# Cross-attention with a snake MLP on one core: batch 4's load, pack and transpose moved forward in a hand-written order, and one square moved to VectorE

## The chip, the cores and the metric

The kernel runs on one core of a Trainium2 chip. The metric is the device time of one execution in microseconds (us), lower being better. The core has five engines that work side by side, each through its own instructions in order: PE (TensorE, matmuls), ACT (ScalarE), DVE (VectorE), POOL (GpSimd) and SP (SyncE, which here only issues DMA transfers). Sixteen DMA engines move the data. An instruction that needs another engine's result waits for it on a semaphore.

## What is computed

Cut to what matters, for B = 8 batches, H = 8 heads, S = 512 tokens, Ns = 32 state rows, D = 64:

```python
scores = scale * np.matmul(x, state.transpose(0, 1, 3, 2))
a = softmax(scores);   xread = np.matmul(a, state)
scores2 = scale * np.matmul(state, x.transpose(0, 1, 3, 2))
a2 = softmax(scores2); sread = np.matmul(a2, x)
attn = np.concatenate([xread, sread], axis=2)      # heads side by side: 4352 rows of 512
h = attn @ w_in                                     # 512 x 2048
s = np.sin(alpha * h)
out = (h + s * s / (alpha + 1e-09)) @ w_out         # 2048 x 512
```

The kernel works in bf16 with float32 accumulation. For `xread` it folds the state into `w_in` (a matrix M for each batch), so that the attention weights, transposed, are multiplied by M directly.

## The kernel before

The whole kernel is a class of small steps and one long string, `ORDER`, that lists them by hand. A step such as `sq.1.13.G` calls the method `sq` with the arguments 1, 13 and "G". The order of the string is the order of the instructions on every engine: each engine takes its own steps from it, and waits where a step needs something that isn't there. Nothing else sets an order. The framework adds the semaphores.

The steps, with t or b for the batch (t = 8 stands for the state rows of all batches), f for one of 16 blocks of 128 columns of the hidden layer:

- `lx.b.0.1`: POOL issues the DMA that loads x of batch b, 512 KB after its cast to bf16, into a tile `xnat` (pool `xpool`, 3 slots, used from batch 1 on).
- `pk.b.0.V`, `pk.b.1.V`: VectorE copies one half of `xnat` into `xp` (5 slots) in another layout. `td.b`: SP issues the DMA transpose of `xp` into `xT` (2 slots). Batch 1 is transposed on PE instead (`xt`, `xc`).
- `sc.b.g`: PE multiplies `xT` with the state into scores; `ex` takes their exponent on ACT; `rs`, `rr` sum and invert on VectorE; `nm` multiplies on POOL, giving the weights A; `ad.b`: SP issues the DMA transpose of A into AT.
- `w`, `cs`, `rc`, `xs`: the second attention (PE, then VectorE). `m` and `me`: M on PE, and its copies to SBUF.
- `h.t.f.bank`: PE multiplies M and AT into one PSUM bank (2 matmuls). `si`: sine on ACT. `sq.t.f.E`: the square on engine E, V for VectorE, A for ACT, G for POOL. `gt`: VectorE multiplies it with 1/alpha and adds h, and so frees the bank of h.
- `o.t.st.f0.f1`: PE multiplies blocks f0 to f1 of gT with w_out for a quarter st of the rows, accumulating in a bank. `oc.t.st.E`: the copy out of that bank. `os.t.st`: SP issues the store.

There are eight PSUM banks, and each `h`, `o`, `sc`, `w` and `m` names the bank it takes; PE has to wait until the bank's last reader is done. A block is the stretch in which a batch's 16 `h` and their squares run. The DMA transposes and the stores share SP's instruction stream, in the order of the string; the loads of x share POOL's with the squares and `nm`.

The change touches lines 52, 62, 64, 69 and 70 of the string. Four places of it, as they were:

```
si.1.13 h.1.15.2 sq.1.3.G gt.1.6 os.0.1 o.0.2.15.16 oc.0.0.A h.1.5.4 sq.1.13.G oc.0.2.V si.1.15
me.2.0.0.V sc.3.1.2 me.2.0.1.A o.1.1.12.13 o.1.3.9.10 xs.0.0 o.1.3.10.11 ex.3.0 o.1.1.13.16 ex.3.1
rr.3.1 h.2.1.3 oc.1.3.V nm.3.1.0.4.G h.2.2.4 h.2.8.1 os.1.3 h.2.3.7 lx.4.0.1 ad.3 si.2.2 o.1.0.0.3.2
sq.2.7.G gt.2.5 o.2.3.1.2 os.1.0 o.2.3.2.3 si.2.6 h.2.10.5 pk.4.1.V pk.4.0.V o.2.3.3.4 sq.2.6.A
o.2.3.4.5 gt.2.7 h.2.11.6 td.4 si.2.10 h.2.12.2 gt.2.6 si.2.11 o.2.0.2.3 sq.2.10.G o.2.0.3.4
```

The multiplication helper `mul` is line 201, so squares on VectorE and POOL, and `nm`, show under L201 in the profile; the copies show under the line of their step. L587 is `o`, L537 `h` (L552 in batch 0, L543 for the state rows), L399 `sc`, L560 `si`, L569 a square on ACT, L576 `gt`, L348 `pk`, L275 the load `lx`, L389 `td`, L440 `ad`, L602 the store.

Of the kernel before, what the change touches and what calls it, by code (L numbers as in the profile page):

```python
# [71 lines left out]
o.2.3.6.7 si.2.13 o.2.0.5.6 sq.2.15.G gt.2.12 o.2.0.6.8 si.2.14 o.2.3.7.9 sq.2.13.A o.2.3.9.10
gt.2.15 sq.2.14.G o.2.0.8.11 gt.2.13 o.2.0.11.12 sc.4.0.5 sc.4.1.6 gt.2.14 o.2.3.10.12 ex.4.0
o.2.3.12.13 w.1.2 cs.1 o.2.0.12.13 rc.1 o.2.3.13.15 ex.4.1 o.2.3.15.16 m.3.0.4.1.3.5 rs.4.0 oc.2.3.A
o.2.0.13.14 me.3.1.0.A o.2.0.14.15 os.2.3 me.3.0.0.V o.2.1.0.1.6 me.3.0.1.A o.2.1.1.2 o.2.0.15.16
rr.4.0 rs.4.1 o.2.1.2.3 me.3.1.1.A nm.4.0.0.4.G h.3.1.0 oc.2.0.A o.2.1.3.4 rr.4.1 xs.1.0
m.3.2.3.4.1.5 si.3.1 nm.4.1.0.4.G os.2.0 xs.1.1 h.3.0.7 me.3.2.0.V h.3.2.2 ad.4 me.3.3.0.V o.2.1.4.6
lx.5.0.1 o.2.2.0.1.3 me.3.3.1.V si.3.2 o.2.2.1.3 si.3.0 h.3.6.1 sq.3.1.V sq.3.2.G me.3.2.1.V
h.3.14.5 si.3.6 o.2.2.3.4 gt.3.1 o.2.2.4.5 sq.3.0.G si.3.14 o.2.2.5.7 gt.3.2 o.2.2.7.8 sq.3.6.A
o.2.2.8.9 h.3.8.4 sq.3.14.G gt.3.0 h.3.5.0 si.3.8 gt.3.6 h.3.15.2 si.3.5 o.2.2.9.10 sq.3.8.G gt.3.14  # L80
o.2.2.10.11 h.3.9.7 si.3.15 h.3.7.1 si.3.9 sq.3.5.G gt.3.8 o.2.2.11.13 si.3.7 h.3.10.5 sq.3.9.G
o.2.2.13.14 sq.3.15.A gt.3.5 o.2.2.14.15 h.3.4.4 si.3.10 gt.3.15 o.2.1.6.7 sq.3.7.G o.2.1.7.8 si.3.4
o.2.2.15.16 o.2.1.8.10 sq.3.10.A gt.3.9 o.2.1.10.11 sq.3.4.G gt.3.7 o.2.1.11.13 oc.2.2.A o.2.1.13.14
gt.3.10 o.2.1.14.16 os.2.2 h.3.3.0 gt.3.4 oc.2.1.A h.3.12.2 si.3.3 pk.5.1.V o.3.2.0.1.7 os.2.1
m.4.2.1.3.5.6 pk.5.0.V si.3.12 sq.3.3.V td.5 o.3.3.0.1.4 me.4.2.1.V me.4.2.0.A o.3.2.1.2 sq.3.12.G
o.3.3.1.2 me.4.3.0.A o.3.2.2.3 gt.3.3 o.3.3.2.3 h.3.11.1 me.4.3.1.A gt.3.12 h.4.10.3 si.3.11 h.4.9.5
si.4.10 h.4.12.0 sq.3.11.V h.4.11.6 si.4.9 gt.3.11 sq.4.10.G o.3.2.3.5 si.4.12 o.3.2.5.7 sq.4.9.A
o.3.2.7.8 gt.4.10 sq.4.12.G o.3.2.8.10 si.4.11 o.3.2.10.11 gt.4.9 o.3.3.3.5 sq.4.11.A o.3.3.5.6
gt.4.12 o.3.3.6.8 m.4.0.2.1.3.5 gt.4.11 o.3.3.8.9 me.4.1.1.V me.4.0.1.A h.3.13.0 me.4.0.0.A h.4.8.6
me.4.1.0.V h.4.15.1 si.3.13 h.4.2.5 si.4.8 sq.3.13.V h.4.1.2 lx.6.0.1 si.4.2 gt.3.13 o.3.2.11.12  # L90
o.3.1.0.2.3 si.4.15 o.3.1.2.3 sq.4.8.V o.3.1.3.4 sq.4.2.G si.4.1 gt.4.8 o.3.3.9.12 sq.4.15.A h.4.3.0
sq.4.1.G gt.4.2 o.3.3.12.13 h.4.13.6 si.4.3 gt.4.15 o.3.3.13.15 si.4.13 sq.4.3.G o.3.3.15.16 gt.4.1
h.4.6.5 oc.3.3.A o.3.2.12.13 h.4.5.1 sq.4.13.G si.4.6 gt.4.3 os.3.3 h.4.14.2 si.4.5 o.3.0.0.1.4
sq.4.6.G o.3.2.13.14 gt.4.13 si.4.14 o.3.0.1.4 sq.4.5.A h.4.4.0 sq.4.14.G gt.4.6 o.3.0.4.5 h.4.0.6
si.4.4 gt.4.5 o.3.1.4.6 si.4.0 sq.4.4.G gt.4.14 o.3.2.14.16 w.2.5 sq.4.0.A pk.6.1.V o.3.1.6.7
oc.3.2.A h.4.7.1 pk.6.0.V gt.4.4 sc.5.0.2 td.6 si.4.7 o.3.1.7.8 sc.5.1.7 gt.4.0 o.3.1.8.9 o.3.0.5.6
ex.5.0 sq.4.7.G o.3.0.6.8 o.3.1.9.11 os.3.2 o.3.0.8.9 gt.4.7 o.3.0.9.12 cs.2 ex.5.1 rs.5.0
m.5.0.0.6.1.2 o.3.0.12.13 rr.5.0 me.5.0.0.A rs.5.1 o.4.3.0.1.7 nm.5.0.0.4.G o.3.0.13.14 me.5.0.1.A
o.3.0.14.15 rr.5.1 o.3.1.11.12 me.5.1.1.V o.3.1.12.13 me.5.1.0.A nm.5.1.0.4.G o.4.3.1.3 rc.2
o.3.0.15.16 o.4.3.3.4 o.3.1.13.14 oc.3.0.A ad.5 o.3.1.14.15 xs.2.0 m.6.0.0.6.2.1 xs.2.1 o.4.3.4.5  # L100
me.6.1.1.V me.6.1.0.A sc.6.1.4 os.3.0 sc.6.0.5 me.6.0.1.A o.4.3.5.6 me.6.0.0.V o.4.3.6.7 ex.6.0
o.4.3.7.8 o.4.0.0.1.2 o.3.1.15.16 ex.6.1 rs.6.0 w.3.1 oc.3.1.A cs.3 rr.6.0 m.5.2.6.0.5.4 rs.6.1
nm.6.0.0.4.G os.3.1 o.4.3.8.9 me.5.2.0.A me.5.2.1.V o.4.0.1.2 o.4.3.9.10 me.5.3.0.A o.4.3.10.11
rr.6.1 o.4.2.0.1.3 rc.3 nm.6.1.0.4.G o.4.2.1.2 me.5.3.1.A h.5.8.6 o.4.3.11.12 xs.3.1 h.5.9.0 si.5.8
ad.6 xs.3.0 o.4.0.2.3 o.4.3.12.14 o.4.2.2.4 h.5.4.5 si.5.9 o.4.3.14.15 sq.5.8.V h.5.3.4 si.5.4
gt.5.8 o.4.2.4.5 sq.5.9.G h.5.0.1 si.5.3 o.4.3.15.16 o.4.0.3.4 si.5.0 sq.5.4.G o.4.2.5.6 oc.4.3.V
o.4.2.6.8 sq.5.3.A gt.5.9 h.5.1.6 os.4.3 sq.5.0.G h.5.5.7 gt.5.4 si.5.1 o.4.2.8.10 si.5.5 gt.5.3
h.5.2.0 sq.5.1.G o.4.2.10.11 gt.5.0 o.4.2.11.12 si.5.2 h.5.14.5 lx.7.0.1 sq.5.5.A gt.5.1 h.6.3.4
o.4.2.12.13 si.5.14 gt.5.5 o.4.2.13.14 sq.5.2.G o.4.0.4.5 o.5.0.0.1.1 si.6.3 o.4.2.14.15 h.6.6.6
sq.5.14.A sq.6.3.G gt.5.2 o.4.0.5.6 h.5.13.7 si.6.6 gt.5.14 o.4.0.6.8 si.5.13 sq.6.6.G o.4.0.8.9  # L110
gt.6.3 o.4.0.9.11 sq.5.13.A o.4.0.11.12 h.6.2.0 gt.6.6 h.5.12.5 si.6.2 gt.5.13 o.4.2.15.16 h.6.4.4
si.5.12 sq.6.2.G o.4.0.12.13 oc.4.2.V o.4.0.13.14 si.6.4 o.4.0.14.15 o.4.1.0.1.6 os.4.2 o.4.1.1.2
sq.5.12.A gt.6.2 sq.6.4.G o.5.0.1.3 o.4.0.15.16 gt.5.12 h.5.10.7 oc.4.0.A o.4.1.2.3 gt.6.4 o.4.1.3.4
si.5.10 o.4.1.4.5 os.4.0 o.4.1.5.6 pk.7.1.V o.4.1.6.7 sq.5.10.A o.4.1.7.8 pk.7.0.V o.4.1.8.10 td.7
gt.5.10 m.6.2.3.0.5.2 o.4.1.10.11 me.6.3.0.V me.6.3.1.A o.4.1.11.12 h.5.7.4 me.6.2.1.A me.6.2.0.V
h.5.11.7 si.5.7 h.5.15.2 si.5.11 h.5.6.5 sq.5.7.V h.6.15.0 si.5.15 gt.5.7 sq.5.11.G o.4.1.12.13
o.5.2.0.1.3 si.5.6 o.5.2.1.3 si.6.15 sq.5.15.G o.4.1.13.14 gt.5.11 o.4.1.14.16 sq.5.6.A h.6.11.4
sq.6.15.G oc.4.1.V h.6.1.7 si.6.11 gt.5.15 o.5.2.3.4 os.4.1 h.6.0.6 si.6.1 sq.6.11.G gt.5.6
o.5.0.3.5 si.6.0 o.5.0.5.6 w.4.2 sq.6.1.A gt.6.15 sq.6.0.G o.5.0.6.7 gt.6.11 o.5.0.7.8 o.5.2.4.5
sc.7.1.5 gt.6.1 sc.7.0.0 o.5.2.5.7 ex.7.0 gt.6.0 o.5.0.8.10 o.5.2.7.8 o.5.1.0.2.4 o.5.0.10.11  # L120
h.6.14.7 ex.7.1 h.6.13.6 rs.7.0 cs.4 si.6.14 rs.7.1 o.5.1.2.4 o.5.0.11.12 rr.7.1 o.5.0.12.13 rc.4
o.5.2.8.9 nm.7.1.0.4.G h.6.10.0 o.5.0.13.14 si.6.13 xs.4.1 o.5.2.9.10 sq.6.14.G o.5.2.10.11 xs.4.0
si.6.10 o.5.2.11.13 h.6.7.5 sq.6.13.A rr.7.0 nm.7.0.0.4.G o.5.2.13.15 si.6.7 h.6.12.2 sq.6.10.A
gt.6.14 gt.6.13 o.5.1.4.5 ad.7 sq.6.7.G o.5.1.5.7 si.6.12 gt.6.10 o.5.1.7.10 sq.6.12.A gt.6.7
o.5.1.10.11 o.5.0.14.15 o.5.1.11.12 gt.6.12 o.5.0.15.16 h.6.5.7 oc.5.0.A o.6.2.0.1.6 h.6.9.0 si.6.5
# [538 lines left out]
```

The softmax here doesn't subtract the row's maximum and nothing guards it: scores larger than these inputs give would overflow.

## Time and profile before

| | |
|---|---|
| time, median of 3 runs | 220.75 us (220.71 to 222.56) |
| span of the profiled execution | 221.2 us |
| busy: PE, ACT, DVE, POOL | 97%, 78%, 73%, 48% |
| lx.4 issued on POOL, for how long | at 63.71 us, 0.94 us |
| pk.4.1 and pk.4.0 on DVE | at 71.73 us, two copies in 0.76 us |
| td.4 issued on SP | at 72.55 us, 1.71 us |
| first scores of batch 4 on PE | at 76.97 us |
| sq.1.13 on POOL | ends at 46.40 us |
| loads of x, from issue to landing | 5.9 least, 7.7 median, 19.6 most |
| transposes into xT, the same | 4.2, 4.3, 5.5 |
| transposes into AT, the same | 3.0, 3.1, 6.8 |

The profile records one execution. Its page gives each engine's busy time, a picture of 40 slices, the chain of waits (followed back from the last instruction to what released each step), and groups of instructions with their mean duration. Other views list who waited for whom, the instructions in order of time (start, duration, engine, line, operation, how many), and the busy time of each engine in chosen stretches. PE's ends are modelled, and weight loads (PEld) overlap with matmuls. Where like instructions follow each other directly, the timeline merges them into one row with a count. A few matmul records are missing.

### The profile page before, as it was taken

The page shows a single profiled execution, that of the slowest core. Times are in us where ns is not written, and L with a number is a line of the kernel's source. Part 1 is how long each engine was busy: PE and PEld are TensorE (multiplying, and loading weights), DVE is VectorE, ACT ScalarE, POOL GpSimd, SP SyncE. Part 2 cuts the span into 40 slices and gives each one's busy share as a digit, 9 for nine tenths or more (in the row PEclk, how much of TensorE's full clock was granted, in tenths as well). Part 3 has the DMA queues.
Part 4 walks back from the last instruction along what each step waited for, and adds up shares of the span by engine and source line. Part 5 has one row for each costly group of instructions (what it writes and reads, how often), then busy time and mean ns, then how long its engine had stood idle before and what let it go on. Part 6 is the DMA issues. An engine that isn't in the chain of part 4 may idle for free.

```text
span 221.2 us, 4330 instructions
## 1 busy us (share of the span) xinstructions
PE 215.7 (97%) x1619; PEld 106.0 (48%) x1619; DVE 162.4 (73%) x286; ACT 173.5 (78%) x297; POOL 107.1 (48%) x115
## 2 busy tenths in 40 slices
...
GB/s 172 198 206 204 205 203 87 174 199 73 119 127 158 96 50 150 44 190 61 81 41 125 126 95 94 108 117 17 47 99 0 98 47 47 0 50 95 1 142 96
DMA packets 38052, 23.48 MB, mean 106 GB/s; under 512 B 20992, under 2 KB 33680, under 8 KB 38032
## 3 DMA queue, kind: packets, MB, share of 16 engines
...
q8 instruction: 12, 0.20, 0.4%
...
## 4 chain that ended last, share of the span: by engine, by line
PE 93%; ACT 3%; DMA 2%; SPq 0%; issue 0%
PE o_ps L587 54%; PE h_ps L537 22%; PE m_ps L488 4%; PE h_ps L543 3%; PE h_ps L552 3%; DMA x<-in_x_dram 2%; PE s_ps L399 2%; PE warm_ps L303 2%; PE w_ps L450 2%; PE w_ps L461 1%; PE x_ps L361 1%; ACT L226 1%; ACT s L560 1%; ACT M L496 1%; PE x_ps L376 0%; PE st_ps L333 0%
## 5 line engine op out<-in xcount | busy, mean ns | idle before, releaser
L587 PE MATMUL o_ps<-w_out_sb,gT 128*128 128x512 bf16 (+2 forms) x560 | 137.7, 373 | 0.0
L576 DVE SCALAR_TENSOR_TENSOR gT<-s,inva_sb,h_ps 128x512 bf16<-128x512 bf16 (+1 forms) x144 | 96.6, 714 | 18.8 <-POOL s L201 9.6
L201 POOL TENSOR_TENSOR s<-s 128x512 bf16<-128x512 bf16 (+1 forms) x76 | 76.7, 1021 | 65.9 <-ACT s L560 62.4
L560 ACT ACTIVATE s<-h_ps,alpha_sb 128x512 bf16<-128x512 f32 (+1 forms) x144 | 88.8, 671 | 10.5 <-PE h_ps L543 4.3
L587 PEld LDWEIGHTS <-gT 128*128 128x128 bf16 x560 | 52.3, 98 | 60.3 <-issue 5.0
L537 PE MATMUL h_ps<-AT,M 128*128 128x512 bf16 x224 | 60.8, 379 | 0.0
L537 PEld LDWEIGHTS <-M 128*128 128x128 bf16 x224 | 21.7, 98 | 25.9 <-issue 0.4
L569 ACT ACTIVATE s<-s 128x512 bf16<-128x512 bf16 (+1 forms) x53 | 31.4, 595 | 0.8
L201 POOL TENSOR_TENSOR A<-E,rR 128x512 bf16<-128x512 bf16 x16 | 16.6, 1048 | 25.7 <-ACT o_sb L595 12.7
L595 ACT COPY o_sb<-o_ps 128x512 f32<-128x512 f32 (+2 forms) x24 | 13.7, 571 | 16.6 <-PE o_ps L587 16.5
L496 ACT CAST M<-m_ps 128x512 bf16<-128x512 f32 x35 | 18.6, 594 | 8.2 <-PE m_ps L488 8.1
L496 DVE CAST M<-m_ps 128x512 bf16<-128x512 f32 x29 | 18.9, 679 | 2.5 <-PE m_ps L488 2.1
L595 DVE COPY o_sb<-o_ps 128x512 f32<-128x512 f32 x11 | 7.6, 691 | 13.0 <-PE o_ps L587 12.9
L303 PE MATMUL warm_ps<-warm 128*128 128x128 bf16 (+3 forms) x66 | 9.9, 295 | 1.4 <-DVE warm L209 1.2
L410 DVE TENSOR_REDUCE R<-E 128x16 f32<-128x512 bf16 x16 | 10.4, 658 | 1.1 <-ACT E L406 0.9
L201 DVE TENSOR_TENSOR s<-s 128x512 bf16<-128x512 bf16 (+1 forms) x15 | 6.2, 415 | 6.8 <-ACT s L560 6.7
L488 PE MATMUL m_ps<-w_in_sb,stT 64*32 64x512 bf16 x256 | 10.2, 382 | 0.0
L468 DVE RECIPROCAL rC<-w_ps 128x128 f32<-128x128 f32 x8 | 7.6, 948 | 3.2 <-PE w_ps L461 3.2
L406 ACT ACTIVATE E<-s_ps 128x512 bf16<-128x512 f32 x16 | 8.8, 601 | 1.4 <-PE s_ps L399 1.3
L552 PE MATMUL h_ps<-AT,M 128*128 128x512 bf16 x32 | 9.4, 380 | 0.4 <-ACT M L496 0.4
L543 PE MATMUL h_ps<-xs_all,w_in_sb 128*128 128x256 bf16 x64 | 9.1, 273 | 0.0
L560 ACT ACT_TABLE_LOAD x5 | 6.4, 1283 | 2.2 <-PE h_ps L537 1.1
...
## 6 DMA issues: line engine op xcount, KB each, us to landing
...
```

The source lines that it names most:

```text
L201: {"V": k.nc.vector, "G": k.nc.gpsimd}[eng].tensor_tensor(out, a, b, ALU.mult)
L303: k.nc.tensor.matmul(wp[:, :cols], k.warm[:, 0:k.P], k.warm[:, :cols], start=True, stop=True)
L488: k.nc.tensor.matmul(k.t["m", b, s + n, g][o0:o0 + k.Ns, :], k.stT[k.half(r), b * k.G + g, c0:c0 + k.Ns], k.w_in_sb[k.half(r), 2 * g + h, ...
L496: k.copy(eng)(k.t["M", b][:, g, s * k.FW:(s + 1) * k.FW], k.t["m", b, s, g][:])
L537: k.nc.tensor.matmul(hp[:, :n], k.t["M", t][:, g, fs], k.t["AT", t][:, g, :], start=(g == 0), stop=(g == k.G - 1),)
L543: k.nc.tensor.matmul(hp[:, :n], k.w_in_sb[:, q, fs], k.xs_all[:, q].rearrange("p b j -> p (b j)"), start=(q == 0), stop=(q == k.Q - 1),)
L552: k.nc.tensor.matmul(k.t["h", t, f][:], k.t["M", t][:, g, f * k.P:(f + 1) * k.P], k.t["AT", t][:, g, :], start=(g == 0), stop=(g == k.G - 1),)
L560: k.nc.scalar.activation(s[:, :n], k.t["h", t, f][:, :n], ACT.Sin, scale=k.alpha_sb[:, f:f + 1])
L569: k.nc.scalar.activation(s2[:, :n], s[:, :n], ACT.Square)
L576: k.nc.vector.scalar_tensor_tensor(gT[:, :n], k.t["s2", t, f][:, :n], k.inva_sb[:, f:f + 1], k.t["h", t, f][:, :n], ALU.mult, ALU.add,)
L587: k.nc.tensor.matmul(k.t["o", t, st, half][:, cols], k.t["gT", t, f][:, rows], k.w_out_sb[:, f, cols], start=(f == 0), stop=(f == k.FT - 1),)
L595: k.copy(eng)(o_sb[:, cols], k.t["o", t, st, half][:, cols])
```

## The change

Three moves in the string, no new code. The load `lx.4.0.1` goes from block 2, where it stood behind the last `nm` of batch 3, to block 1, behind `sq.1.3.G` and so between the transposes `td.2` and `td.3`. To make up for it on POOL, the square `sq.1.13` goes to VectorE. The packs `pk.4.1.V` and `pk.4.0.V` and the transpose `td.4` go from block 2 to the place behind `xs.0.0`, ahead of `ex.3`, `rs.3`, `nm.3` and of `ad.3`, the transpose of batch 3's weights. PE's own steps keep their order. The rest of the diff is re-wrapping of lines.

```diff
-si.1.13 h.1.15.2 sq.1.3.G gt.1.6 os.0.1 o.0.2.15.16 oc.0.0.A h.1.5.4 sq.1.13.G oc.0.2.V si.1.15
...
+si.1.13 h.1.15.2 sq.1.3.G lx.4.0.1 gt.1.6 os.0.1 o.0.2.15.16 oc.0.0.A h.1.5.4 sq.1.13.V oc.0.2.V
...
-me.2.0.0.V sc.3.1.2 me.2.0.1.A o.1.1.12.13 o.1.3.9.10 xs.0.0 o.1.3.10.11 ex.3.0 o.1.1.13.16 ex.3.1
-rs.3.0 o.1.3.11.13 oc.1.1.A o.1.3.13.14 rr.3.0 h.2.0.0 rs.3.1 nm.3.0.0.4.G os.1.1 o.1.3.14.16 si.2.0
-rr.3.1 h.2.1.3 oc.1.3.V nm.3.1.0.4.G h.2.2.4 h.2.8.1 os.1.3 h.2.3.7 lx.4.0.1 ad.3 si.2.2 o.1.0.0.3.2
...
-sq.2.7.G gt.2.5 o.2.3.1.2 os.1.0 o.2.3.2.3 si.2.6 h.2.10.5 pk.4.1.V pk.4.0.V o.2.3.3.4 sq.2.6.A
-o.2.3.4.5 gt.2.7 h.2.11.6 td.4 si.2.10 h.2.12.2 gt.2.6 si.2.11 o.2.0.2.3 sq.2.10.G o.2.0.3.4
...
+me.2.0.0.V sc.3.1.2 me.2.0.1.A o.1.1.12.13 o.1.3.9.10 xs.0.0 pk.4.1.V pk.4.0.V td.4 o.1.3.10.11
+ex.3.0 o.1.1.13.16 ex.3.1 rs.3.0 o.1.3.11.13 oc.1.1.A o.1.3.13.14 rr.3.0 h.2.0.0 rs.3.1 nm.3.0.0.4.G
+os.1.1 o.1.3.14.16 si.2.0 rr.3.1 h.2.1.3 oc.1.3.V nm.3.1.0.4.G h.2.2.4 h.2.8.1 os.1.3 h.2.3.7 ad.3
...
+oc.1.0.A h.2.6.3 sq.2.7.G gt.2.5 o.2.3.1.2 os.1.0 o.2.3.2.3 si.2.6 h.2.10.5 o.2.3.3.4 sq.2.6.A
+o.2.3.4.5 gt.2.7 h.2.11.6 si.2.10 h.2.12.2 gt.2.6 si.2.11 o.2.0.2.3 sq.2.10.G o.2.0.3.4 o.2.3.5.6
```

More of the change, by code (lines that the diff above doesn't have):

```diff
@@ L51 @@
 h.1.3.0 si.1.6 gt.1.0 o.0.1.14.16 si.1.3 sq.1.6.G h.1.13.6 gt.1.1 oc.0.1.A o.0.2.14.15 o.0.0.15.16
-si.1.13 h.1.15.2 sq.1.3.G gt.1.6 os.0.1 o.0.2.15.16 oc.0.0.A h.1.5.4 sq.1.13.G oc.0.2.V si.1.15
-h.1.7.3 os.0.0 gt.1.3 o.1.1.0.1.5 si.1.5 os.0.2 h.1.8.1 sq.1.15.G gt.1.13 o.1.1.1.2 si.1.7
+si.1.13 h.1.15.2 sq.1.3.G lx.4.0.1 gt.1.6 os.0.1 o.0.2.15.16 oc.0.0.A h.1.5.4 sq.1.13.V oc.0.2.V
+si.1.15 h.1.7.3 os.0.0 gt.1.3 o.1.1.0.1.5 si.1.5 os.0.2 h.1.8.1 sq.1.15.G gt.1.13 o.1.1.1.2 si.1.7
 o.1.2.0.2.7 sq.1.5.A o.1.1.2.3 sq.1.7.G h.1.12.0 gt.1.15 si.1.8 h.1.9.6 gt.1.5 o.1.2.2.3 si.1.12
@@ L61 @@
 m.2.0.3.4.0.2 ad.2 rc.0 o.1.3.7.8 me.2.1.1.A o.1.3.8.9 sc.3.0.7 xs.0.1 me.2.1.0.A o.1.1.11.12 os.1.2
-me.2.0.0.V sc.3.1.2 me.2.0.1.A o.1.1.12.13 o.1.3.9.10 xs.0.0 o.1.3.10.11 ex.3.0 o.1.1.13.16 ex.3.1
-rs.3.0 o.1.3.11.13 oc.1.1.A o.1.3.13.14 rr.3.0 h.2.0.0 rs.3.1 nm.3.0.0.4.G os.1.1 o.1.3.14.16 si.2.0
-rr.3.1 h.2.1.3 oc.1.3.V nm.3.1.0.4.G h.2.2.4 h.2.8.1 os.1.3 h.2.3.7 lx.4.0.1 ad.3 si.2.2 o.1.0.0.3.2
-si.2.8 sq.2.0.V o.1.0.3.4 sq.2.2.G gt.2.0 h.2.4.5 si.2.1 o.1.0.4.6 si.2.3 sq.2.8.G o.1.0.6.7 gt.2.2
@@ L66 @@
-h.2.9.6 si.2.4 o.2.3.0.1.0 o.1.0.7.8 sq.2.1.G o.1.0.8.9 sq.2.3.A gt.2.8 o.1.0.9.10 h.2.5.4 si.2.9
-gt.2.3 o.1.0.10.11 sq.2.4.G o.1.0.11.12 si.2.5 h.2.7.1 gt.2.1 o.1.0.12.13 sq.2.9.A sq.2.5.G
-o.1.0.13.14 gt.2.4 o.1.0.14.15 si.2.7 o.1.0.15.16 o.2.0.0.1.7 gt.2.9 o.2.0.1.2 oc.1.0.A h.2.6.3
-sq.2.7.G gt.2.5 o.2.3.1.2 os.1.0 o.2.3.2.3 si.2.6 h.2.10.5 pk.4.1.V pk.4.0.V o.2.3.3.4 sq.2.6.A
-o.2.3.4.5 gt.2.7 h.2.11.6 td.4 si.2.10 h.2.12.2 gt.2.6 si.2.11 o.2.0.2.3 sq.2.10.G o.2.0.3.4
-o.2.3.5.6 si.2.12 h.2.15.4 h.2.13.1 sq.2.11.A gt.2.10 sq.2.12.G o.2.0.4.5 si.2.15 h.2.14.3 gt.2.11
@@ L72 @@
[L72 to L125, printed above, removed]
@@ L126 @@
-os.5.0 o.5.2.15.16 o.5.1.12.13 si.6.9 sq.6.5.V o.5.1.13.14 o.6.2.1.2 oc.5.2.V o.5.3.0.1.5 sq.6.9.A
+me.2.0.0.V sc.3.1.2 me.2.0.1.A o.1.1.12.13 o.1.3.9.10 xs.0.0 pk.4.1.V pk.4.0.V td.4 o.1.3.10.11
+ex.3.0 o.1.1.13.16 ex.3.1 rs.3.0 o.1.3.11.13 oc.1.1.A o.1.3.13.14 rr.3.0 h.2.0.0 rs.3.1 nm.3.0.0.4.G
+os.1.1 o.1.3.14.16 si.2.0 rr.3.1 h.2.1.3 oc.1.3.V nm.3.1.0.4.G h.2.2.4 h.2.8.1 os.1.3 h.2.3.7 ad.3
+si.2.2 o.1.0.0.3.2 si.2.8 sq.2.0.V o.1.0.3.4 sq.2.2.G gt.2.0 h.2.4.5 si.2.1 o.1.0.4.6 si.2.3
+sq.2.8.G o.1.0.6.7 gt.2.2 h.2.9.6 si.2.4 o.2.3.0.1.0 o.1.0.7.8 sq.2.1.G o.1.0.8.9 sq.2.3.A gt.2.8
@@ new lines @@
+o.1.0.9.10 h.2.5.4 si.2.9 gt.2.3 o.1.0.10.11 sq.2.4.G o.1.0.11.12 si.2.5 h.2.7.1 gt.2.1 o.1.0.12.13
+sq.2.9.A sq.2.5.G o.1.0.13.14 gt.2.4 o.1.0.14.15 si.2.7 o.1.0.15.16 o.2.0.0.1.7 gt.2.9 o.2.0.1.2
+oc.1.0.A h.2.6.3 sq.2.7.G gt.2.5 o.2.3.1.2 os.1.0 o.2.3.2.3 si.2.6 h.2.10.5 o.2.3.3.4 sq.2.6.A
+o.2.3.4.5 gt.2.7 h.2.11.6 si.2.10 h.2.12.2 gt.2.6 si.2.11 o.2.0.2.3 sq.2.10.G o.2.0.3.4 o.2.3.5.6
+si.2.12 h.2.15.4 h.2.13.1 sq.2.11.A gt.2.10 sq.2.12.G o.2.0.4.5 si.2.15 h.2.14.3 gt.2.11 o.2.3.6.7
+si.2.13 o.2.0.5.6 sq.2.15.G gt.2.12 o.2.0.6.8 si.2.14 o.2.3.7.9 sq.2.13.A o.2.3.9.10 gt.2.15
@@ new lines @@
+sq.2.14.G o.2.0.8.11 gt.2.13 o.2.0.11.12 sc.4.0.5 sc.4.1.6 gt.2.14 o.2.3.10.12 ex.4.0 o.2.3.12.13
+w.1.2 cs.1 o.2.0.12.13 rc.1 o.2.3.13.15 ex.4.1 o.2.3.15.16 m.3.0.4.1.3.5 rs.4.0 oc.2.3.A o.2.0.13.14
+me.3.1.0.A o.2.0.14.15 os.2.3 me.3.0.0.V o.2.1.0.1.6 me.3.0.1.A o.2.1.1.2 o.2.0.15.16 rr.4.0 rs.4.1
+o.2.1.2.3 me.3.1.1.A nm.4.0.0.4.G h.3.1.0 oc.2.0.A o.2.1.3.4 rr.4.1 xs.1.0 m.3.2.3.4.1.5 si.3.1
+nm.4.1.0.4.G os.2.0 xs.1.1 h.3.0.7 me.3.2.0.V h.3.2.2 ad.4 me.3.3.0.V o.2.1.4.6 lx.5.0.1 o.2.2.0.1.3
@@ new lines @@
+me.3.3.1.V si.3.2 o.2.2.1.3 si.3.0 h.3.6.1 sq.3.1.V sq.3.2.G me.3.2.1.V h.3.14.5 si.3.6 o.2.2.3.4
+gt.3.1 o.2.2.4.5 sq.3.0.G si.3.14 o.2.2.5.7 gt.3.2 o.2.2.7.8 sq.3.6.A o.2.2.8.9 h.3.8.4 sq.3.14.G
+gt.3.0 h.3.5.0 si.3.8 gt.3.6 h.3.15.2 si.3.5 o.2.2.9.10 sq.3.8.G gt.3.14 o.2.2.10.11 h.3.9.7 si.3.15
+h.3.7.1 si.3.9 sq.3.5.G gt.3.8 o.2.2.11.13 si.3.7 h.3.10.5 sq.3.9.G o.2.2.13.14 sq.3.15.A gt.3.5
+o.2.2.14.15 h.3.4.4 si.3.10 gt.3.15 o.2.1.6.7 sq.3.7.G o.2.1.7.8 si.3.4 o.2.2.15.16 o.2.1.8.10
+sq.3.10.A gt.3.9 o.2.1.10.11 sq.3.4.G gt.3.7 o.2.1.11.13 oc.2.2.A o.2.1.13.14 gt.3.10 o.2.1.14.16
@@ new lines @@
+os.2.2 h.3.3.0 gt.3.4 oc.2.1.A h.3.12.2 si.3.3 pk.5.1.V o.3.2.0.1.7 os.2.1 m.4.2.1.3.5.6 pk.5.0.V
+si.3.12 sq.3.3.V td.5 o.3.3.0.1.4 me.4.2.1.V me.4.2.0.A o.3.2.1.2 sq.3.12.G o.3.3.1.2 me.4.3.0.A
+o.3.2.2.3 gt.3.3 o.3.3.2.3 h.3.11.1 me.4.3.1.A gt.3.12 h.4.10.3 si.3.11 h.4.9.5 si.4.10 h.4.12.0
+sq.3.11.V h.4.11.6 si.4.9 gt.3.11 sq.4.10.G o.3.2.3.5 si.4.12 o.3.2.5.7 sq.4.9.A o.3.2.7.8 gt.4.10
+sq.4.12.G o.3.2.8.10 si.4.11 o.3.2.10.11 gt.4.9 o.3.3.3.5 sq.4.11.A o.3.3.5.6 gt.4.12 o.3.3.6.8
+m.4.0.2.1.3.5 gt.4.11 o.3.3.8.9 me.4.1.1.V me.4.0.1.A h.3.13.0 me.4.0.0.A h.4.8.6 me.4.1.0.V
@@ new lines @@
+h.4.15.1 si.3.13 h.4.2.5 si.4.8 sq.3.13.V h.4.1.2 lx.6.0.1 si.4.2 gt.3.13 o.3.2.11.12 o.3.1.0.2.3
+si.4.15 o.3.1.2.3 sq.4.8.V o.3.1.3.4 sq.4.2.G si.4.1 gt.4.8 o.3.3.9.12 sq.4.15.A h.4.3.0 sq.4.1.G
+gt.4.2 o.3.3.12.13 h.4.13.6 si.4.3 gt.4.15 o.3.3.13.15 si.4.13 sq.4.3.G o.3.3.15.16 gt.4.1 h.4.6.5
+oc.3.3.A o.3.2.12.13 h.4.5.1 sq.4.13.G si.4.6 gt.4.3 os.3.3 h.4.14.2 si.4.5 o.3.0.0.1.4 sq.4.6.G
+o.3.2.13.14 gt.4.13 si.4.14 o.3.0.1.4 sq.4.5.A h.4.4.0 sq.4.14.G gt.4.6 o.3.0.4.5 h.4.0.6 si.4.4
+gt.4.5 o.3.1.4.6 si.4.0 sq.4.4.G gt.4.14 o.3.2.14.16 w.2.5 sq.4.0.A pk.6.1.V o.3.1.6.7 oc.3.2.A
@@ new lines @@
+h.4.7.1 pk.6.0.V gt.4.4 sc.5.0.2 td.6 si.4.7 o.3.1.7.8 sc.5.1.7 gt.4.0 o.3.1.8.9 o.3.0.5.6 ex.5.0
+sq.4.7.G o.3.0.6.8 o.3.1.9.11 os.3.2 o.3.0.8.9 gt.4.7 o.3.0.9.12 cs.2 ex.5.1 rs.5.0 m.5.0.0.6.1.2
+o.3.0.12.13 rr.5.0 me.5.0.0.A rs.5.1 o.4.3.0.1.7 nm.5.0.0.4.G o.3.0.13.14 me.5.0.1.A o.3.0.14.15
+rr.5.1 o.3.1.11.12 me.5.1.1.V o.3.1.12.13 me.5.1.0.A nm.5.1.0.4.G o.4.3.1.3 rc.2 o.3.0.15.16
+o.4.3.3.4 o.3.1.13.14 oc.3.0.A ad.5 o.3.1.14.15 xs.2.0 m.6.0.0.6.2.1 xs.2.1 o.4.3.4.5 me.6.1.1.V
+me.6.1.0.A sc.6.1.4 os.3.0 sc.6.0.5 me.6.0.1.A o.4.3.5.6 me.6.0.0.V o.4.3.6.7 ex.6.0 o.4.3.7.8
@@ new lines @@
+o.4.0.0.1.2 o.3.1.15.16 ex.6.1 rs.6.0 w.3.1 oc.3.1.A cs.3 rr.6.0 m.5.2.6.0.5.4 rs.6.1 nm.6.0.0.4.G
+os.3.1 o.4.3.8.9 me.5.2.0.A me.5.2.1.V o.4.0.1.2 o.4.3.9.10 me.5.3.0.A o.4.3.10.11 rr.6.1
+o.4.2.0.1.3 rc.3 nm.6.1.0.4.G o.4.2.1.2 me.5.3.1.A h.5.8.6 o.4.3.11.12 xs.3.1 h.5.9.0 si.5.8 ad.6
+xs.3.0 o.4.0.2.3 o.4.3.12.14 o.4.2.2.4 h.5.4.5 si.5.9 o.4.3.14.15 sq.5.8.V h.5.3.4 si.5.4 gt.5.8
+o.4.2.4.5 sq.5.9.G h.5.0.1 si.5.3 o.4.3.15.16 o.4.0.3.4 si.5.0 sq.5.4.G o.4.2.5.6 oc.4.3.V o.4.2.6.8
+sq.5.3.A gt.5.9 h.5.1.6 os.4.3 sq.5.0.G h.5.5.7 gt.5.4 si.5.1 o.4.2.8.10 si.5.5 gt.5.3 h.5.2.0
```

19 lines of the change are left out of this document (added).

## The prediction, written before the change was run

> **What bounds the kernel now.** I read the page first, then the chain of waits, then a table of 10 us stretches, and last the timeline around the moved steps. The page and the chain:
>
> ```profile
> span 221.2 us, 4330 instructions
> PE 215.7 (97%) x1619; PEld 106.0 (48%) x1619; DVE 162.4 (73%) x286; ACT 173.5 (78%) x297; POOL 107.1 (48%) x115
> ...
> PE 93%; ACT 3%; DMA 2%; SPq 0%; issue 0%
> PE o_ps L587 54%; PE h_ps L537 22%; PE m_ps L488 4%; PE h_ps L543 3%; PE h_ps L552 3%; DMA x<-in_x_dram 2%; PE s_ps L399 2%; PE warm_ps L303 2%; PE w_ps L450 2%; PE w_ps L461 1%; PE x_ps L361 1%; ACT L226 1%; ACT s L560 1%; ACT M L496 1%; PE x_ps L376 0%; PE st_ps L333 0%
> ```
>
> A busy PE alone proves little, because its ends are modelled. So I count starts: in the chain a run of 10 matmuls of 512 columns takes 2.16 us, one each 0.216 us. From 20 us to the last matmul the starts follow each other at this pace without a hole (the largest are 0.1 us, at changes to smaller matmuls), and the waits of PE between 20 and 203 us are an empty list. The 3% of ACT and 2% of DMA in the chain lie in the first 20 us, ahead of everything the change touches. **PE is the path**, and its order of steps is not changed. A gain would need a hole to close, and there is none.
>
> The place where the old order is late shows in two waits, and where the load now goes shows in the stretches:
>
> ```profile
> DVE xp L348 <- DMA xnat<-in_x_dram: 0.8, 1, 0.8
> ...
> PEld L399 <- DMA xT<-xp: 0.2, 1, 0.2
> ```
>
> ```profile
> 47.00:48.00 1.00, 1.00 (x6) 0.42 (x5) 0.76 (x2) 1.00 (x3) 1.00 (x2) 1.00 0.89 291
> 48.00:53.00 5.00, 5.00 (x38) 2.50 (x37) 5.00 (x10) 4.98 (x9) 4.71 (x5) 1.00 0.00 0
> 53.00:54.00 1.00, 1.00 (x6) 0.49 (x5) 1.00 (x2) 0.99 (x2) 0.04 (x1) 1.00 0.62 124
> ```
>
> In the stretches the last two columns are the DMA share and GB/s: from 48 to 53 us the DMA engines are empty. VectorE waits 0.8 us for batch 4's x, and the weight load of batch 4's scores waits 0.2 us for its transpose. But the matmul behind it does not start late: the six `o` matmuls before it start at 75.68 and end their turn at 75.68 + 6 x 0.216 = 76.97, where the scores start.
>
> **What the skill says.** The Trainium skill, "SBUF — State Buffer", section "Who interferes with whom": a VectorE instruction with two SBUF inputs and a GpSimd one that reads SBUF lock each other out, and the later one waits. The trace is mixed: sq.4.8.V, begun first, took its usual 0.42 us beside a POOL square begun 0.23 us later; a pack at 112.92 us, begun under a POOL square, took 0.59 in place of 0.42. "DMA: Bandwidth & Descriptors", section "Issuing engines are not separate DMA queues": loads issued by POOL and transposes issued by SP share the same engines and interleave. The trace agrees: AT transposes land 3.1 us after issue at the median, the one issued at 83.58 beside a load of x took 6.8. "Perfetto Trace Analysis", section "Identifying the Most-Contended Engine", warns against PE's busy share; hence the count of starts.
>
> **Part 1, the load lx.4 in block 1.** It goes on POOL behind sq.1.3.G, in place of sq.1.13.G.
>
> ```profile
> 44.36 2.04 POOL L201 TENSOR_TENSOR s<-s 128x512 bf16<-128x512 bf16 x2
> ```
>
> ```profile
> 45.19 0.69 DVE L595 COPY o_sb<-o_ps 128x512 f32<-128x512 f32 x1
> 45.79 1.40 DVE L576 SCALAR_TENSOR_TENSOR gT<-s,inva_sb,h_ps 128x512 bf16<-128x512 bf16 x2
> ```
>
> The POOL row holds two squares, sq.1.3.G and sq.1.13.G, 1.00 us apart; the VectorE rows are oc.0.2, then gt.1.3 and gt.1.13. An issue costs POOL 0.94 us (the row of the loads) and about 0.1 to the next square (63.71 + 0.94 = 64.65, next square 64.76). So POOL is 1.04 - 1.00 = 0.04 us later at sq.1.15.G: nothing, since gt.1.15 has 0.9 us before PE needs its bank. The slot of xnat that it fills was batch 1's, last read by the transposes on PE at about 28.7 us, so it needn't wait. The load lands 5.9 (quiet) to 8.0 us (the old lx.4) after issue: 45.4 + 5.9 to 8.0 = 51.3 to 53.4. It shares with the stores of batch 0 until 48 and then has the empty stretch. td.3 is issued at 52.21 and its traffic begins at 53: a touch of the tail at most. td.3 takes 4.3 and its scores are due at 58.8, so over 2 us are spare. Cost: 0.
>
> **Part 2, sq.1.13 on VectorE.** 0.43 us (the row of such squares: 415 ns at the mean with shorter ones, 0.42 to 0.43 for 512 columns), between gt.1.6 and oc.0.2. Its input, the sine si.1.13, is there at 45.06 (ACT 44.35 + 0.70), so VectorE doesn't wait. Queued behind are oc.0.2, gt.1.3, gt.1.13, gt.1.15 and on. They go 0.43 us later until VectorE's next idle time, 0.24 us before gt.1.15 at 47.43; then 0.19 remain, until an idle 0.13 at 54.2 and 1.25 at 57.9 us. Who waits: gt.1.13 is the second of the two at 45.79 and ends at 47.19; it frees the bank of h.1.9, the second of two steps that start at 47.36, so 47.79. **Margin 0.60, less 0.43: 0.17 us.** oc.0.2 and gt.1.3 have 0.83, gt.1.5 0.68, gt.1.8 0.54 against 0.19. Is 0.17 enough? PE ran through a margin of 0.19 at 42.61 (oc.0.3 ended at 42.42). If the port lock holds VectorE until sq.1.3.G ends at 45.40, 0.21 us are added, and PE is late by 0.21 - 0.17 = 0.04, or 0.21 if the whole 0.17 is latency. Below nothing is excluded: nothing on PE gets earlier. I take 0.05 of 0 to 0.25.
>
> **Part 3, pk.4 and td.4 ahead of ad.3.** The two packs (0.34 + 0.42 = 0.76 us) go behind xs.0.0, which ends at 60.25 us, with the load 7 us landed. VectorE idles 0.36 there, so rs.3.0 starts at 61.04 in place of 60.60: 0.44 late. Behind it stand rr.3, rs.3.1 and oc.1.3; POOL's nm.3.0 and nm.3.1 wait for rr.3 and end at 64.2 in place of 63.76. An idle 0.94 us at 63.2 swallows it on VectorE; on POOL the removed issue (0.94) does, so the next square, due at 64.76, is on time. oc.1.3 frees a bank for which PE has 2.8 us. On SP, td.4 waits for pk.4.0 (61.04) and issues for 1.7 us, to 62.8. Queued behind it: os.1.1 (61.60 before, now 62.8), os.1.3 (63.22, now about 63.7) and ad.3 (63.79, now 64.2). Two stores half a microsecond to a microsecond late: six o_sb buffers, no waiter near. ad.3 is needed by h.3.1 at 81.8 us and lands by about 69 even beside td.4. td.4 lands at about 65.4, 11 us ahead of its scores at 76.97. Its slot of xT was batch 2's, last read at 52.7. Cost: 0.
>
> **Part 4, what leaves block 2.** 0.76 us of VectorE and 0.8 of waiting go at 71 to 72.5 us; next late there is POOL's square for gt.2.7 and the sines behind it. PE had no hole there: the margins (h.2.13 and h.2.14 at 0.37) grow. Gain: 0 on PE.
>
> **Sum.** 221.2 + 0 + 0.05 + 0 + 0 = 221.25 us for the profiled execution. Its span is 0.45 above the median of the runs shown, 220.75, and inside their spread (220.71 to 222.56), so I subtract 0.45: **220.8 us**.
>
> **Rivals.**
> - *The likeliest (0.60):* PE keeps its pace, 220.6 to 221.0, forecast 220.8.
> - *A small new stall (0.20):* the 0.17 margin is broken, and one or two behind it (gt.1.8, ad.2, which has 0.97 at h.2.0). For it: several margins under 0.4 us in a row. Against: each stall only moves PE once, the others then have more time. 0.2 to 1.2 us: 221.0 to 222.0.
> - *A small gain (0.10):* modelled PE ends hide the 0.2 us wait at batch 4's scores and margins in block 2. 220.3 to 220.6; more would need holes that the starts don't show.
> - *The load meets td.3 (0.10), on the slower side.* If lx.4 still moves after about 54.5 us, td.3 is stretched. Taking the worst transpose (6.8 for 3.1, so 3.7 more), it lands at 60.15 for scores whose weights load at 58.60: 1.55 us of stall. ad.2 then follows at 60.15 + 3.1 = 63.25 for h.2.0, due at 62.99: 0.26 more, in all 222.6. With ad.2 stretched by 3.7 as well, 226.3. For it: the old loads all took 7.3 us or more beside a transpose. Against: the five empty microseconds.
> - *It doesn't do what it says:* a wait on the xnat slot holds the load. Its readers ended 17 us earlier; counted into the first two.
>
> **Numbers.** About 1% (2.2 us) is what counts as told from no change. Faster by that needs 2.2 us of holes: 0.02. Slower: 0.08 of the collision and 0.02 of unseen stalls, 0.10. Within: 0.88. The range runs from the gain's 220.4 to the small stall's end, 222.0; it leaves out most of the collision.
>
> **What would show it.** The load's issue near 45.4 and landing before 53.5; no wait for xnat before the packs; td.4 issued near 61 and landed near 65.4; the 0.2 us wait of the scores gone; PE's start of h.1.9 still at 47.8 and of h.2.0 at 61.4. I am wrong if PE's waits list td.3, ad.2 or VectorE between 45 and 65 us, or if PE's starts show a pace other than 0.216.

## The result, and the profile after

The changed kernel takes 221.32 us (median of 22 runs, 220.85 to 221.9), the kernel before 221.16 (22 runs, 220.56 to 222.96). The ratio of the means is 0.9999, 95% interval 0.9984 to 1.0013: no change, and any there was is under 0.2%.

The page of the changed kernel, first its size and engines, then the chain of waits:

```profile
span 219.2 us, 4303 instructions
PE 211.4 (96%) x1593; PEld 104.5 (48%) x1619; DVE 162.9 (74%) x287; ACT 173.4 (79%) x297; POOL 106.2 (48%) x114
...
PE 90%; DMA 6%; POOL 1%; issue 1%; ACT 0%
PE o_ps L587 54%; PE h_ps L537 22%; DMA w_in_sb<-in_moe_w_in_dram 5%; PE m_ps L488 4%; PE h_ps L543 3%; PE h_ps L552 2%; PE w_ps L450 2%; PE s_ps L399 2%; PE w_ps L461 1%; DMA s<-in_state_dram 1%; POOL w_in_sb L282 1%; PE x_ps L376 0%; POOL st_nat L267 0%; POOL s01b L255 0%; ACT o_sb L595 0%
```

The span is 2.0 us shorter than the 221.2 of before, which looks like a gain and isn't one. Two landmarks on PE separate the start from the rest: the step m.1.3 at the end of the start, and h.8.14, the last h. The timeline of PE (start, duration, engine, line, operation), before:

```profile
32.76 0.41 PE L488 MATMUL m_ps<-w_in_sb,stT 64*32 64x512 bf16 x8
...
203.21 0.60 PE L543 MATMUL h_ps<-xs_all,w_in_sb 128*128 128x256 bf16 x4
```

and after:

```profile
30.78 0.41 PE L488 MATMUL m_ps<-w_in_sb,stT 64*32 64x512 bf16 x8
...
201.23 0.60 PE L543 MATMUL h_ps<-xs_all,w_in_sb 128*128 128x256 bf16 x4
```

Both distances are 170.45 us, and nearly every landmark between them (the m, scores, w, cs and state-row steps, whose records are complete) is 1.98 us earlier after than before, to the hundredth. PE did not gain or lose anything in the stretch that the change touches. The 1.98 us lie ahead of it, in the first 20 us; experiment e0 takes them up. (Some 26 matmul records are missing in the trace of after; PE's busy time is lower for that reason alone.) To compare places, 1.98 is added to a time of after.

The rows of VectorE and POOL at the moved square and load, after; first VectorE (gt.1.1 and gt.1.6, the square, oc.0.2, then gt.1.3, gt.1.13 and gt.1.15), then POOL:

```profile
41.67 1.53 DVE L576 SCALAR_TENSOR_TENSOR gT<-s,inva_sb,h_ps 128x512 bf16<-128x512 bf16 x2
43.12 0.58 DVE L201 TENSOR_TENSOR s<-s 128x512 bf16<-128x512 bf16 x1
43.62 0.68 DVE L595 COPY o_sb<-o_ps 128x512 f32<-128x512 f32 x1
44.22 2.05 DVE L576 SCALAR_TENSOR_TENSOR gT<-s,inva_sb,h_ps 128x512 bf16<-128x512 bf16 x3
```

```profile
41.38 2.04 POOL L201 TENSOR_TENSOR s<-s 128x512 bf16<-128x512 bf16 x2 [0.19 <-ACT s L560]
43.36 0.94 POOL L275 DMA_DIRECT2D xnat<-in_x_dram  x1
44.32 2.09 POOL L201 TENSOR_TENSOR s<-s 128x512 bf16<-128x512 bf16 x2
```

The square starts 0.30 us before POOL's square ends (41.38 + 2.04 = 43.42) and takes 0.58 in place of 0.43: it was held for 0.15. Its start overlaps the end of gt.1.6, so that oc.0.2 behind it starts at 43.62 (45.60), 0.41 us later than before. The load is issued at 43.36 (45.34 in the time of before) and lands 8.2 us later, at 53.5. And SP, where td.3, td.4 and ad.3 are the three rows:

```profile
50.29 1.83 SPq L389 DMA_TRANSPOSE xT<-xp  x1
...
59.00 1.93 SPq L389 DMA_TRANSPOSE xT<-xp  x1
...
62.54 1.30 SPq L440 DMA_TRANSPOSE AT<-A  x1
```

td.4 is issued at 59.00 (60.98) and lands at 63.83, for scores that start at 75.00. The waits for the load and for td.4 are gone from the list.

### The profile page after: what moved, and what is told of

Read it like the earlier page. It is cut to its first block, busy times and chain, and to the rows that moved or that the text cites. A ratio compares the mean times of both kernels' runs of the same rounds, so it can differ in the third digit from the quotient of the medians.

```text
span 219.2 us, 4303 instructions
## 1 busy us (share of the span) xinstructions
PE 211.4 (96%) x1593; PEld 104.5 (48%) x1619; DVE 162.9 (74%) x287; ACT 173.4 (79%) x297; POOL 106.2 (48%) x114
## 4 chain that ended last, share of the span: by engine, by line
PE 90%; DMA 6%; POOL 1%; issue 1%; ACT 0%
PE o_ps L587 54%; PE h_ps L537 22%; DMA w_in_sb<-in_moe_w_in_dram 5%; PE m_ps L488 4%; PE h_ps L543 3%; PE h_ps L552 2%; PE w_ps L450 2%; PE s_ps L399 2%; PE w_ps L461 1%; DMA s<-in_state_dram 1%; POOL w_in_sb L282 1%; PE x_ps L376 0%; POOL st_nat L267 0%; POOL s01b L255 0%; ACT o_sb L595 0%
## 5 line engine op out<-in xcount | busy, mean ns | idle before, releaser
L587 PE MATMUL o_ps<-w_out_sb,gT 128*128 128x512 bf16 (+2 forms) x542 | 133.9, 373 | 1.6 <-issue 1.0
L201 POOL TENSOR_TENSOR s<-s 128x512 bf16<-128x512 bf16 (+1 forms) x75 | 75.9, 1022 | 64.4 <-ACT s L560 62.7
L537 PE MATMUL h_ps<-AT,M 128*128 128x512 bf16 x219 | 60.0, 379 | 0.3
L201 DVE TENSOR_TENSOR s<-s 128x512 bf16<-128x512 bf16 (+1 forms) x16 | 7.0, 439 | 6.2 <-ACT s L560 6.1
L303 PE MATMUL warm_ps<-warm 128*128 128x128 bf16 (+3 forms) x66 | 8.6, 271 | 1.4 <-DVE warm L209 1.2
L552 PE MATMUL h_ps<-AT,M 128*128 128x512 bf16 x29 | 8.4, 379 | 0.9 <-ACT M L496 0.7
L543 PEld LDWEIGHTS <-w_in_sb 128*128 128x128 bf16 x64 | 6.3, 98 | 3.4
```

The costliest lines, as they stand in the source:

```text
L201: {"V": k.nc.vector, "G": k.nc.gpsimd}[eng].tensor_tensor(out, a, b, ALU.mult)
L537: k.nc.tensor.matmul(hp[:, :n], k.t["M", t][:, g, fs], k.t["AT", t][:, g, :], start=(g == 0), stop=(g == k.G - 1),)
L543: k.nc.tensor.matmul(hp[:, :n], k.w_in_sb[:, q, fs], k.xs_all[:, q].rearrange("p b j -> p (b j)"), start=(q == 0), stop=(q == k.Q - 1),)
L552: k.nc.tensor.matmul(k.t["h", t, f][:], k.t["M", t][:, g, f * k.P:(f + 1) * k.P], k.t["AT", t][:, g, :], start=(g == 0), stop=(g == k.G - 1),)
L587: k.nc.tensor.matmul(k.t["o", t, st, half][:, cols], k.t["gT", t, f][:, rows], k.w_out_sb[:, f, cols], start=(f == 0), stop=(f == k.FT - 1),)
```

## The experiments

All are judged by the distance from m.1.3 to h.8.14, 170.45 us in both kernels, since the start differs from one execution to the next. Seven kernels ran.

**e0: the kernel before, once more.** No edit.

> The kernel before, unchanged, profiled once more. Theory (the 2.0 us between the profiled spans of before and after come from the first 20 us and differ from execution to execution, not from kernel to kernel): m.1.3 to h.8.14 is 170.45 again, and m.1.3 starts somewhere between 30.4 and 32.8 us, as it has in the runs so far, with the span 188.4 us longer than that start. Rival (the change shortens the start): m.1.3 at 32.7 to 32.8 again.

Span 219.1 us, time 221.0, m.1.3 at 30.61, distance 170.52, and 188.5 us from m.1.3 to the end. The start belongs to the execution, not to the kernel: in the nine profiles m.1.3 starts at 30.5 to 31.1 us in eight and at 32.76 in the one shown of before. The rival falls.

What differs in the start is the pace of PE. It transposes x in four groups of four matmuls (L361). The last group in the execution shown of before, then in e0:

```profile
9.32 0.63 PE L361 MATMUL x_ps<-ident,xp 128*128 128x128 bf16 x4
...
7.72 0.39 PE L361 MATMUL x_ps<-ident,xp 128*128 128x128 bf16 x4
```

In the execution shown of before all four groups take 0.61 to 0.63 us. In the other eight profiles a group takes 0.39 or 0.40 from 7.1 us on at the latest. From the second group to the transposes of the state (L333), which stand behind the fourth, 4.53 us pass in before and 2.74 in e4, where all groups are quick. Yet the last cast of x on ACT, which the groups read, ends at 7.76 us in before and at 7.62 in e4. So about 1.8 of the 2 us are matmuls that ran slower, not a transfer that came later.

**e1: the load and the square alone.**

```diff
-xs.0.0 pk.4.1.V pk.4.0.V td.4 o.1.3.10.11
+xs.0.0 o.1.3.10.11
...
-h.2.10.5 o.2.3.3.4 sq.2.6.A o.2.3.4.5 gt.2.7 h.2.11.6 si.2.10
+h.2.10.5 pk.4.1.V pk.4.0.V o.2.3.3.4 sq.2.6.A o.2.3.4.5 gt.2.7 h.2.11.6 td.4 si.2.10
```

> The changed kernel with its third move undone: the load of batch 4's x stays in block 1 and the square on VectorE, but the two packs and td.4 go back to block 2. Measure: PE's time from the start of m.1.3 to the start of h.8.14, its last step of h; it is 170.45 us both before (32.76 to 203.21) and after (30.78 to 201.23), wherever the first 20 us ended. Theory (PE keeps its pace, the moves only shift slack): 170.45 within 0.05, no wait of VectorE for the load before the packs, td.4 issued about 1 us earlier than before, since the packs no longer wait 0.8 us. Rival (two effects cancel: the VectorE square costs some tenths and the early transpose gives them back): 170.6 to 170.9 here, with the gain missing.

Distance 170.48, ratio to before 1.0003 (0.9985 to 1.0021). No cancelling: the move of the packs and td.4 is worth nothing, and so are the other two together. The packs no longer wait for x, and td.4 goes out 1.0 us earlier than before (71.57 against 72.55 in the time of before). One row was not foreseen, VectorE's two packs:

```profile
68.28 0.96 DVE L348 COPY xp<-xnat 128x1024 bf16<-128x1024 bf16 x2
```

0.96 us for the pair in place of 0.76. They now start under a POOL square that ends 0.34 us later.

**e2: the square left on POOL.**

```diff
-sq.1.13.V oc.0.2.V
+sq.1.13.G oc.0.2.V
```

> The changed kernel with sq.1.13 left on POOL, behind the load. Theory (the margin of gt.1.13 to h.1.9 is what counts, 0.60 us before, 0.20 after): POOL ends sq.1.13 about 1.0 us later than before, gt.1.13 follows, so that h.1.9 starts 0.35 to 0.5 us late and the scores of batch 2 perhaps 0.1 more; m.1.3 to h.8.14 is 170.8 to 171.1. Rival (POOL's order does not matter, PE has other work): 170.45.

Distance 172.73: 2.28 us lost, four times what was expected. The waits of PE from 20 to 203 us:

```profile
PE s_ps L399 <- DVE gT L576: 1.7, 1, 1.7
...
PE h_ps L537 <- DVE gT L576: 0.2, 1, 0.2
```

The second wait is h.1.9's. PE's row of h.1.12 and h.1.9 before, then the one of h.1.9 in e2:

```profile
47.36 1.03 PE L537 MATMUL h_ps<-AT,M 128*128 128x512 bf16 x4
...
46.25 0.59 PE L537 MATMUL h_ps<-AT,M 128*128 128x512 bf16 x2 [0.23 <-DVE gT L576]
```

h.1.9 is the second half of the first row, so it starts at 47.79; in e2 it starts at 46.25, 48.18 in the time of before. That is 0.39 us late, within the 0.35 to 0.5 expected. (The list shows less, because it counts from the modelled end of the matmul before.) The 1.7 at the scores of batch 2 is something else; VectorE's rows and POOL's show it:

```profile
46.44 2.06 DVE L576 SCALAR_TENSOR_TENSOR gT<-s,inva_sb,h_ps 128x512 bf16<-128x512 bf16 x3 [0.24 <-POOL s L201]
48.42 2.25 DVE L348 COPY xp<-xnat 128x1024 bf16<-128x1024 bf16 x1
50.59 2.05 DVE L576 SCALAR_TENSOR_TENSOR gT<-s,inva_sb,h_ps 128x512 bf16<-128x512 bf16 x3
```

```profile
46.37 5.20 POOL L201 TENSOR_TENSOR s<-s 128x512 bf16<-128x512 bf16 x5
```

The pack pk.3.1, 0.42 us in the kernel before and 0.41 after, takes 2.25. It starts while the third of five POOL squares runs and ends 0.3 us after the fourth. In this kernel POOL is late, so all its inputs are ready and the five follow each other without a gap; in the kernel before POOL waited 0.1 us for a sine between two of them, and pk.3.1 slipped in there. The load of x isn't what slows the pack: it is under way beside the same pack after, too.

**e6: e2 with that pack moved away**, to where POOL turns to issuing the load.

```diff
-sq.1.13.G oc.0.2.V
+sq.1.13.G pk.3.1.V oc.0.2.V
...
-pk.3.1.V h.1.11.4
+h.1.11.4
```

> The kernel of e2 (load in block 1, sq.1.13 left on POOL) with one step moved: the pack pk.3.1 on VectorE, which took 2.25 us there in place of 0.42 beside three POOL squares in a row, is done earlier, ahead of oc.0.2, where POOL turns to issuing the load. Theory (the 2.28 us of stall in e2 are not the late square, but a pack that is locked out of its port while POOL's squares follow each other without a gap): the wait for gt.1.8 at the scores of batch 2 (1.73 us in e2) is gone, the one at h.1.9 stays, m.1.3 to h.8.14 is 170.65 to 171.0. Rival (the late square itself drives the stall, through the squares and gT behind it): the wait for gt.1.8 stays above 1 us and the distance above 171.8.

Distance 170.92; of PE's two waits only the 0.2 us at h.1.9 is left. The packs on VectorE:

```profile
43.23 0.58 DVE L348 COPY xp<-xnat 128x1024 bf16<-128x1024 bf16 x1
...
50.48 1.26 DVE L348 COPY xp<-xnat 128x1024 bf16<-128x1024 bf16 x1
```

The moved one takes 0.58, the other, pk.3.0, now under a full POOL square, 1.26, where PE can bear it. So most of e2's loss was the locked-out pack, 172.73 - 170.92 = 1.81 us, and 0.47 the late square: 0.39 at h.1.9, and 0.08 behind the scores of batch 2. The rival falls.

**e3: the kernel before with the load issued where the transposes move data.**

```diff
-h.2.3.7 lx.4.0.1 ad.3
+h.2.3.7 ad.3
...
-sq.1.14.G o.1.1.7.8
+sq.1.14.G lx.4.0.1 o.1.1.7.8
```

> The kernel before with one thing moved: the load of batch 4's x is issued behind the last square of block 1 (about 53 us), where POOL is idle, so that it moves data while td.3 and ad.2 do. Rival of the prediction put to the test (a load that meets the transposes holds up PE): td.3 lands up to 3.7 us later than the usual 4.3 after its issue and ad.2 6.8 in place of 3.0; sc.3.0 up to 1.5 us late, h.2.0 2 to 3 us late; m.1.3 to h.8.14 is 172 to 175.5, time 0.8 to 2.3% more. If transposes keep their time beside a load: 170.45 and no change.

Distance 171.94, time 222.91, ratio 1.0063 (1.0042 to 1.0084). td.3 lands 6.4 us after its issue (4.2 before), ad.2 5.35 (3.0 before). td.3's delay of 2.15 us just fits into the room it had and PE loses nothing at sc.3.0; ad.2's doesn't, and PE waits:

```profile
PE h_ps L537 <- DMA AT<-A: 1.3, 1, 1.3
```

h.2.0 starts 1.49 us late. So the mechanism of the slower rival is real, at about half of the price that the worst transpose of before suggested, and at ad.2, not at td.3. In its place in the change the load meets the empty stretch from 48 to 53 us instead, and costs nothing.

**e4: the square three times.**

```diff
-sq.1.13.V oc.0.2.V
+sq.1.13.V sq.1.13.V sq.1.13.V oc.0.2.V
```

> The changed kernel with the square sq.1.13 on VectorE done three times, so that the suspected cost is tripled (the last result is used). Theory: two more squares are 0.86 us; gt.1.13 has 0.20 us to spare, so PE stalls 0.66 us at h.1.12 and h.1.9 together and m.1.3 to h.8.14 is 171.1 to 171.25. Rival (PE has more slack than the margins say): 170.45 to 170.6.

Distance 171.16, 0.71 more; 0.66 was foreseen. VectorE's row of the squares, and PE's of h.1.12 and h.1.9:

```profile
43.46 1.25 DVE L201 TENSOR_TENSOR s<-s 128x512 bf16<-128x512 bf16 x3
```

```profile
46.02 1.25 PE L537 MATMUL h_ps<-AT,M 128*128 128x512 bf16 x4
```

The row of PE starts at 47.66 in the time of before, 0.30 us late, and its four matmuls take 1.25 us in place of 1.03: h.1.9 waits inside it. By h.1.9, 0.52 us are lost, the other 0.19 at the scores of batch 2. The two more squares took 0.67 us (1.25 less 0.58), not 0.86; less the margin of 0.2 that is 0.47, close to the 0.52. So the margin is real, and that the total came out as foreseen is in part luck.

**e5: the kernel before with the packs of batch 4 two microseconds later.**

```diff
-h.2.10.5 pk.4.1.V pk.4.0.V o.2.3.3.4 sq.2.6.A o.2.3.4.5 gt.2.7 h.2.11.6 td.4 si.2.10 h.2.12.2 gt.2.6
+h.2.10.5 o.2.3.3.4 sq.2.6.A o.2.3.4.5 gt.2.7 h.2.11.6 si.2.10 h.2.12.2 gt.2.6 pk.4.1.V pk.4.0.V td.4
```

> The kernel before with the packs of batch 4 and td.4 moved later in block 2, behind gt.2.6, about 2 us after their old place. Theory (before, td.4 landed just when PE needed it, 0.15 us to spare, so the old place was at the edge): td.4 is issued at about 74.5 and lands at about 78.8, the scores of batch 4 start 1.9 to 2.1 us late, m.1.3 to h.8.14 is 172.3 to 172.6, time 0.8 to 1.0% more. Rival (later steps of PE fill in or the wait is absorbed): under 171.

Distance 174.44 in the profiled execution, twice the loss foreseen; time 224.24 (median of 4 runs, 223.38 to 224.95), ratio 1.0125 (1.0101 to 1.0148). PE waits 2.3 us for td.4, so that the scores start 2.44 us late, a little more than expected, because the two packs took 2.46 us beside POOL's squares. The other 1.55 us come after the wait. The stretches around it (length, then busy time of PE, PEld, DVE, ACT and POOL with counts, PE's granted clock, DMA share, GB/s):

```profile
75.00:77.25 2.25, 0.01 (x1) 0.00 (x0) 1.86 (x3) 0.56 (x1) 0.00 (x0) 1.00 0.84 157
77.25:78.00 0.75, 0.67 (x17) 0.60 (x19) 0.00 (x0) 0.28 (x1) 0.00 (x0) 1.00 0.00 0
78.00:79.00 1.00, 1.00 (x8) 0.52 (x8) 0.00 (x0) 0.81 (x2) 0.00 (x0) 0.54 0.06 16
79.00:80.00 1.00, 1.00 (x21) 0.91 (x20) 0.00 (x0) 0.00 (x0) 0.00 (x0) 0.50 0.00 0
80.00:81.00 1.00, 1.00 (x10) 0.37 (x5) 0.63 (x1) 0.00 (x0) 0.00 (x0) 0.50 0.00 0
81.00:82.00 1.00, 1.00 (x11) 0.29 (x17) 0.88 (x2) 0.07 (x1) 0.00 (x0) 0.75 0.00 0
```

PE stands still from 75.0 to 77.3 us, and from 78 to 81.5 its granted clock is halved: 3.4 us at half speed can account for the 1.55 us. But that belongs to this execution. It is the longest of the four (224.95 us) and its mean granted clock is 0.992, which 3.4 us at half clock in 223.1 make; in the other three the mean is 1.000. One of 33 executions of the kernel before also has 0.992 (223.17 us), and the profile of that kernel shows no wait of PE behind the start. So the halving follows the wait here, but that the wait caused it isn't shown. The cost that is seen to come from the late packs is the 2.44 us, and without the halving the other three still take 2.2 to 3.3 us more than the median before, 221.16.

The old place of the packs was at an edge. The changed kernel has 11 us of room there instead.

## Why the prediction was right, and where a step was off

- **PE as the path, with no hole to close:** right. 170.45 us before and after, and every delay put into another engine beyond its margin (e2, e3, e4, e5) came out on PE.
- **Part 1, the load:** right. Issued at 45.34 (forecast 45.4), landed at 53.5 (51.3 to 53.4, so 0.1 late), td.3 landed at 56.52 against 56.45. A td.3 that lands 2 us later, as in e3, would still have been free at sc.3.0; the danger was ad.2. POOL's cost was 0.04 in the sum and the square behind the load is in fact 0.05 earlier.
- **Part 2, the square:** right in place and size. VectorE is 0.40 us late at gt.1.13 (forecast 0.43), the margin at h.1.9 is 0.20 (0.17), PE doesn't stall (0.05 taken). The lock by POOL's square held the square for 0.15 of the 0.21 allowed, and the overlap with its neighbours hid that. What the prediction did not see is what the square's move is for: it priced POOL with the square gone and did not ask what a POOL without gaps does to the packs. e2 and e6 give the answer, 1.8 us.
- **Part 3, packs and td.4 ahead of ad.3:** right. rs.3.0 is 0.24 us late (forecast 0.44; the packs overlap their neighbours' ends), ad.3 0.73 us (0.4), without effect.
- **Part 4:** right. The wait of 0.2 us of the weight load was not on PE's path; without it (after, e1) the distance is the same.
- **The sum:** its last step was wrong in its reasoning. It set the span of the profiled execution, 221.2, against the times of the runs and subtracted 0.45. But a time is longer than its span: 221.22 to 219.2 after, 221.0 to 219.1 in e0, so 1.9 to 2.0 us (1.8 to 2.3 in all runs on record). By that the execution shown of before took an estimated 223.1 us, about 2 above the median, all of it ahead of m.1.3. The forecast did not suffer from this, since what is left after the subtraction is the median of the three runs, 220.75, and the 0.05. It suffered from that median: it is 0.41 below the 221.16 of 22 runs. With 221.16 and the 0.05 the sum gives 221.2 for the measured 221.32. As it stood, the measured time lay outside the 220.6 to 221.0 of the likeliest case and inside the 221.0 to 222.0 of the small stall, though no stall came: the change in PE's time was right, the level it was added to was not.
- **The rivals:** the small gain and the small stall didn't come. The collision did not happen, and e3 shows that it would have with the load 7.6 us later. It costs 1.5 us there, at h.2.0; the prediction's 1.55 were for sc.3.0, which loses nothing, so the likeness of the two numbers is chance.

What stays open: why PE's first matmuls ran slow for longer in the execution shown of before. The views give its granted clock as 1.00 there, and no run here changed it.
